# Batch 0's first attention block in a new order: three tokens of q and k first, products of ones in the pauses, g loaded as rows, and the late FFN tiles moved on

## The chip, the cores and the metric

The kernel runs on one core of a Trainium2 chip. Time is the device time of one execution in microseconds; the median of several runs counts. Within the core, TensorE (PE) multiplies matrices and transposes, VectorE (DVE) and ScalarE (ACT) work element by element, GpSimd (POOL) issues most loads and adds, SyncE (SP) issues loads and stores.

## The reference

Squared-relu attention over 8 batches, 12 heads, 448 positions and 64 elements a head, followed by a layer norm and a two-layer FFN with a residual:

```python
scores = (1 / sqrt(64)) * q @ k.T                  # per batch and head
attn   = maximum(scores, 0) ** 2 / 448
x      = (attn @ v), heads side by side            # 8 x 448 x 768
xn     = (x - mean(x)) / sqrt(var(x) + 1e-6) * g   # g: moe_g_ln, 768
out    = x + maximum(xn @ w_ch1, 0) @ w_ch2        # w_ch1 768 x 3072, w_ch2 3072 x 768
```

All inputs and outputs are float32 in HBM.

## The kernel before

**Tiling.** A position is p * 7 + j: 64 values of p on partitions, 7 of j, called tokens or slots here. Each batch is three groups of four heads (G = 3); a group's q and k are tiles of 128 partitions with two rows of 448 elements, and its transposes are 7 pairs of 64x128 blocks for q and as many for k. The loads by POOL's queue cast to bf16 on the way. The 1/std of the layer norm is applied after the second FFN product, so FFN1 needs only the centred x times g (tile xc).

**The first two batches** are worked in two blocks of query tokens each: BLK = (0..2, 3..6) for batch 0, (0..3, 4..6) for batch 1. A block goes over the three groups: transposes (L205 on PE, copies out of PSUM at L209 by DVE and ACT), scores (L307) two key slots at a time, relu on ACT (L318), square on DVE (L296), the product with v (L337), the scaled copy into xT (L344) and, times g, into xc (L350 on DVE; L348 on ACT for groups 1 and 2 of the very first block). At the end `centre` sums over the 768 columns with a product with ones (L385) and subtracts the mean (L391). Then FFN1 of that block (24 tiles `ni` of 128 columns: `ffn1_head` for 0 to 2 at L540, `ffn1` at L518) runs interleaved with the attention units of the next block, by `interleave(main, side, free, ahead)`: it runs `ahead` side units first, then spreads the others over the main units but the last `free`. From batch 2 on both batches of a pair are worked whole; this part isn't touched.

**The order is written by hand** (manual_schedule): each engine runs its instructions in the order in which the program issues them, and waits only where data or a buffer requires it. PSUM has three buffers of two banks (ps_sc: scores, value products, idle_ps) and two of one bank (ps_mm: FFN1 tiles, batch 0's transposes, the busy products).

**Loads.** q and k of batch 0, group 0 come uncast as float32 into `stage` on the queues of SP and ACT (L150), and are cast by DVE (q, tokens 0 to 2), ACT (k) and POOL (q, tokens 3 to 6) at L158. Everything else early goes in order through POOL's queue: q and k of groups 1 and 2, v of groups 0 to 2, the six column blocks of w1 in two halves each (`load_w1`, L138; block i holds tiles 4i to 4i+3), then batch 1's q, k and v (L120). A load on this queue waits for the load eight places before it. g is read as single elements into 128 partitions by six columns, in two loads on SP's queue (L177); `scale_g` (L182, L183) makes g_mean and g_score of it on DVE and is issued before the first block's third unit.

**Products without a use.** `idle(n)` issues n products of 128x128 ones into idle_ps, `busy(n)` n products of 128x448 into a ps_mm buffer. Their results are never read:

```python
idle(30)                                   # before the first transposes
for _ in range(n):                         # busy(n), L283
    nc.tensor.matmul(ps[:, :S], ones, qbuf[0][:, D:D + S], start=True, stop=True)
```

Of the kernel before, what the change touches and what calls it, by code (L numbers as in the profile page):

```python
# [12 lines left out]
def interleave(main, side, free=0, ahead=0):  # L13


    for unit in side[:ahead]:
        unit()
    side = side[ahead:]
    n, done = len(main) - free, 0
    for i, unit in enumerate(main):  # L20
        unit()
        want = min(len(side), (len(side) * (i + 1)) // n)
        while done < want:
            side[done]()
            done += 1
# [3 lines left out]
def kernel(  # L29
# [22 lines left out]
    nc = tc.nc  # L52
    P = 128
    HP = 64
    bf16 = mybir.dt.bfloat16
    fp32 = mybir.dt.float32

    B, H, S, D = q.shape
# [3 lines left out]
    J = S // HP  # L62
    NP = H // 2
    G = NP // 2
# [28 lines left out]
    nc.vector.memset(ones, 1.0)  # L93


    srcs = {
        n: [t[b].rearrange("(r hh) (p j) d -> (hh p) r (j d)", hh=2, p=HP) for b in range(B)]
        for n, t in (("q", q), ("k", k), ("v", v))
# [9 lines left out]
    def load(n, names):  # L108
        if n >= len(groups):
            return  # L110
        b, m = groups[n]
        for name in names:
            if b == 1 and name != "v":
                o = (2 * m + "qk".index(name)) * 2 * S
                t = hold[:, o:o + 2 * S].rearrange("p (r s) -> p r s", r=2)
            elif name == "q":
                t = qbuf[m][:, D:D + 2 * S].rearrange("p (r s) -> p r s", r=2)
            else:
                t = io.tile([P, 2, S], bf16, tag=name, name=name + "_sb", bufs=4 if name == "v" else 3)
            nc.gpsimd.dma_start(t, srcs[name][b][:, m:NP:G, :])  # L120
            qkv[name, b, m] = t
# [21 lines left out]

    stage = hpool.tile([P, K2, S2], bf16, tag="hT", name="stage_sb")
    stage = stage.rearrange("p a n -> p (a n)")[:, :8 * S].bitcast(fp32)
    stage = stage.rearrange("p (i r s) -> p i r s", i=2, r=2)
    for i, (queue, name) in enumerate(((nc.sync, "q"), (nc.scalar, "k"))):
        queue.dma_start(stage[:, i], srcs[name][0][:, 0:NP:G, :])  # L150

    nc.scalar.activation(spool.tile([P, 1], fp32, tag="root", name="root"), eps_sb, ACTF.Sqrt)
    qkv["q", 0, 0] = qbuf[0][:, D:D + 2 * S].rearrange("p (r s) -> p r s", r=2)
# [2 lines left out]
    def cast(copy, name, lo, hi):  # L156
        s = slice(lo * D, hi * D)
        copy(qkv[name, 0, 0][:, :, s], stage[:, "qk".index(name), :, s])  # L158

    load(1, "qk")  # L160
    make_identity(nc, identity)
    load(2, "qk")
    load(0, "v")
    load(1, "v")
    load(2, "v")
    cast(nc.gpsimd.tensor_copy, "q", 3, J)
    for i in range(6):
        load_w1(i)
    load(3, "qkv")
    load(4, "qk")  # L170
    load(5, "qk")

    g_sb = const.tile([P, K1], fp32)
    g_src = moe_g_ln.rearrange("(hf c p) -> hf p c", hf=2, p=HP)
    with nc.allow_non_contiguous_dma(reason="one vector of 768"):
        for hf in range(2):
            nc.sync.dma_start(g_sb[hf * HP:(hf + 1) * HP, :], g_src[hf])  # L177
    g_mean = const.tile([P, K1], fp32)
    g_score = const.tile([P, K1], fp32)

    def scale_g():
        nc.vector.tensor_scalar_mul(g_mean, g_sb, -1.0 / d_model)  # L182
        nc.vector.tensor_scalar_mul(g_score, g_sb, score_scale)  # L183

# [3 lines left out]
    def idle(n):  # L188

        for _ in range(n):  # L190
            nc.tensor.matmul(idle_ps[:, 0, :P], ones, ones, start=True, stop=True)

    xT, xc = {}, {}
    st = {}

    def piece(sb, b, m, n, cuts):
        if b == 0:
            ps = ps_mm.tile([P, 1024], bf16, tag="mm", name="tr_ps")
        else:
            ps = ps_sc.tile([P, 2, 1024], bf16, tag="sc", name="tr_ps")[:, 0]  # L200
        src, i = qkv[n, b, m], "qk".index(n)
        for copy, lo, hi in cuts:
            for j in range(lo, hi):
                for pr in range(2):
                    nc.tensor.transpose(  # L205
                        ps[pr * HP:(pr + 1) * HP, j * P:(j + 1) * P],
                        src[:, pr, j * D:(j + 1) * D], identity)
        for copy, lo, hi in cuts:
            copy(sb[:, i * J + lo:i * J + hi, :],  # L209
                 ps[:, lo * P:hi * P].rearrange("p (j c) -> p j c", c=P))  # L210

    def transposes(b, m):


        if b == 0:
            o = 12 * 1024 + m * 2 * J * P
            sb = early[:, o:o + 2 * J * P].rearrange("p (i c) -> p i c", c=P)
        elif m:
            o = (m - 1) * 2 * J * P
            sb = hold[:, o:o + 2 * J * P].rearrange("p (i c) -> p i c", c=P)  # L220
        else:
            sb = tpool.tile([P, NB, P], bf16, tag="qT", name="qT_sb", bufs=3)
        dve, act = nc.vector.tensor_copy, nc.scalar.copy
        if (b, m) == (0, 0):

            cast(dve, "q", 0, 3)
            cast(act, "k", 0, 3)
            cast(act, "k", 3, J)
            idle(30)
            piece(sb, b, m, "q", ((dve, 0, 3),))  # L230
            idle(2)
            piece(sb, b, m, "k", ((dve, 0, 3), (dve, 3, J)))
            idle(3)
        elif b == 0:
            piece(sb, b, m, "q", ((dve, 0, J),))
            piece(sb, b, m, "k", ((dve, 0, 3), (act, 3, J)))
        else:
            piece(sb, b, m, "q", ((dve, 0, J),))
            piece(sb, b, m, "k", ((dve, 0, J),))
        squares_now()  # L240
        st[b, m] = {
            "q": lambda i, r: sb[:, 0:J],
            "k": lambda i: sb[:, J + i],
            "where": lambda pr, j: (j, pr),
            "attn": [], "sb": sb}
# [25 lines left out]


    FULL = (0, J)
    BLK = (((0, 3), (3, J - 3)), ((0, 4), (4, J - 4)))
    FIRST = (0, BLK[0][0])
    n_early = [0]

    def busy(n):


        ps = ps_mm.tile([P, 512], fp32, tag="mm", name="busy_ps")
        for _ in range(n):
            nc.tensor.matmul(ps[:, :S], ones, qbuf[0][:, D:D + S], start=True, stop=True)  # L283

    def of(blk, b=0):
        o = b % 2 * S
# [4 lines left out]
    def squares_now(n=None):  # L291


        if n is None or n in [k for k, _ in later]:
            for _, a in later:
                nc.vector.tensor_mul(a, a, a)  # L296
            later.clear()
# [99 lines left out]
    def transposed(n):  # L397

        if groups[n][0] < by_dma:
            transposes(*groups[n])  # L400
            return


        if n > by_dma * G:
            load(n + 2, "kq")
        keys_dma(n)
        queries_dma(n)

    def attention_block(b, blk):


        lo, hi, first = b * G, b * G + G, blk[0] == 0
        units = [lambda: transposed(lo)] if first else []

        def unit(n, part):
            squares_now()
            for i in range(4 * part, min(4 * part + 4, J), 2):
                if (b, blk) == FIRST and (n == G - 1 or n and i == 2):
                    busy(1)
                scores(n, tuple(range(i, min(i + 2, J))), blk)  # L420
            if (b, blk) == FIRST and part and n == hi - 1:
                squares_now()
            if b == 1 and not first and part and n == hi - 1:
                transposed(hi)
            if part and n > lo:
                values(n - 1, blk)
                if not first:
                    load(n + 3, "v")
        for n in range(lo, hi):
            units.append(lambda n=n: unit(n, 0))  # L430
            if first and n + 1 < hi:
                units.append(lambda n=n: transposed(n + 1))
            units.append(lambda n=n: unit(n, 1))

        def last():
            if (b, blk) == FIRST:
                piece(st[0, 0]["sb"], 0, 0, "q", ((nc.scalar.copy, 3, J),))
            values(hi - 1, blk)
            if (b, blk) == FIRST:
                busy(2)  # L440
            if b == 1 and not first:
                load(hi + 3, "v")
        units.append(last)
        units.append(lambda: centre(b, blk))
        return units

    def attention(bs):

# [159 lines left out]


    pairs = B // 2  # L610
    for i, unit in enumerate(attention_block(0, BLK[0][0])):
        if i == 2:
            scale_g()
        unit()
    interleave(ffn1_units(0, BLK[0][0]), attention_block(0, BLK[0][1]), 3, 1)
    w2 = wpool.tile([P, K2, d_model], bf16, tag="w2", name="w2")
    for i in range(4):
        load_w2(w2, i, 4)
    load(6, "qkv")
    load(7, "qk")  # L620
    load(8, "qk")
    interleave(ffn1_units(0, BLK[0][1]), attention_block(1, BLK[1][0]), 3, 1)
    interleave(ffn1_units(1, BLK[1][0]), attention_block(1, BLK[1][1]), 3, 1)
    tokens(0)
    transposed(by_dma * G + 1)
# [46 lines left out]
```

## Time and profile before

| | |
|---|---|
| timed runs (3) | median 549.29 us, 549.14 to 549.51 |
| profiled execution | 552.11 us, its span 550.3 us |
| PE busy in the span | 540.8 us |
| DVE, ACT, POOL busy | 266.4, 260.4, 109.5 us |
| HBM read, written | 51.91 MB, 11.01 MB |
| mean granted PE clock | 0.991 |
| first product of FFN1 (L540) | starts at 24.42 us |

The span is counted from the first instruction to the last. An engine's busy time leaves out its waits and its issuing of DMAs; PE's products are pipelined, so that a busy PE needn't be at its peak. PEclk is the share of TensorE's full clock that was granted. All times of instructions below are from the span's start.

### The profile page before, as it was taken

How to read it: one execution, taken by the hardware profiler on the slowest of the kernel's cores; microseconds unless marked ns; L12 is line 12 of the kernel's file. 1: busy time of each engine (PE TensorE's matmuls, PEld its weight loads, DVE VectorE, ACT ScalarE, POOL GpSimd, SP SyncE). 2: the span in 40 equal slices, each digit the busy share in tenths (PEclk: the TensorE clock that was granted, in tenths of full speed). 3: DMA queues.
4: the chain of work that ended last, by engine and by line, in shares of the span. 5: the costliest groups of instructions: out<-in, count | busy, mean ns of one | idle time of the engine just before them, and what ended most of it. 6: DMA issues, size and time to landing. Idle time of an engine off the chain costs nothing.

```text
span 550.3 us, 11108 instructions
## 1 busy us (share of the span) xinstructions
PE 540.8 (98%) x4734; PEld 320.1 (58%) x4734; DVE 266.4 (48%) x511; ACT 260.4 (47%) x424; POOL 109.5 (20%) x135
## 2 busy tenths in 40 slices
PE   6999999999999999999999999999999999999997
PEld 4688778755555555555555555555555555556665
DVE  3686754268897241047787551016687680001111
ACT  3776676565543444455445244445555254440000
POOL 7334102115524200002534400001230400000000
PEclk7899999999999999999999999999999999999999
DMA  9999999999999960018998960005931140001212
GB/s 187 205 206 208 211 170 143 151 165 145 154 157 147 182 53 0 1 30 135 162 168 138 174 115 1 0 15 84 145 81 31 45 101 0 1 0 44 58 43 58
DMA packets 111539, 56.64 MB, mean 103 GB/s; under 512 B 78081, under 2 KB 111489, under 8 KB 111489
## 3 DMA queue, kind: packets, MB, share of 16 engines
q0 software_dynamic: 26976, 25.50, 32.3%
q1 hardware_dynamic: 84000, 29.77, 30.8%
q8 instruction: 37, 0.61, 0.4%
q10 hardware_dynamic: 512, 0.66, 0.3%
q14 instruction: 14, 0.11, 0.1%
HBM read 51.91 MB, written 11.01 MB: 114 GB/s over the span
## 4 chain that ended last, share of the span: by engine, by line
PE 96%; DMA 2%; ACT 1%; DVE 1%; SPq 0%; issue 0%; DVEq 0%
PE o_ps L554 39%; PE h_ps L518 39%; PE sc_ps L307 7%; PE av_ps L337 6%; DMA g_sb<-in_moe_g_ln_dram 2%; PE o_ps L581 1%; PE h_ps L540 1%; PE sum_ps L385 1%; PE tr_ps L205 1%; ACT early L318 1%; DVE early L296 0%; ACT early L209 0%; SPq L177 0%; ACT xc_sb L348 0%; DVE early L209 0%; DVE hT_sb L524 0%
## 5 line engine op out<-in xcount | busy, mean ns | idle before, releaser
L554 PE MATMUL o_ps<-w,hT_sb 128*128 128x384 bf16 x1296 | 219.6, 326 | 0.0
L518 PE MATMUL h_ps<-xc_sb,w 128*128 128x448 bf16 (+2 forms) x1368 | 219.0, 318 | 0.4 <-DVE hT_sb L524 0.4
L518 PEld LDWEIGHTS <-w 128*128 128x128 bf16 x1368 | 128.7, 98 | 86.4 <-issue 2.7
L554 PEld LDWEIGHTS <-hT_sb 128*128 128x128 bf16 x1296 | 123.1, 98 | 93.4 <-issue 15.2
L318 ACT ACTIVATE attn_sb<-sc_ps 128x896 bf16<-128x896 f32 (+4 forms) x150 | 126.4, 902 | 87.8 <-PE sc_ps L307 71.3
L526 ACT ACTIVATE hT_sb<-h_ps 128x448 bf16<-128x448 f32 (+2 forms) x212 | 102.7, 484 | 120.9 <-PE h_ps L518 120.5
L320 DVE TENSOR_TENSOR attn_sb<-attn_sb 128x896 bf16<-128x896 bf16 x126 | 81.7, 653 | 40.3 <-ACT attn_sb L318 39.0
L565 DVE SCALAR_TENSOR_TENSOR o_sb<-o_ps,rstd_sb,xtok_sb 128x384 f32<-128x384 f32 (+1 forms) x57 | 34.4, 604 | 56.4 <-PE o_ps L554 49.8
L503 DVE RECIPROCAL rstd_sb<-rstd_sb 128x1 f32<-128x1 f32 (+1 forms) x10 | 1.7, 168 | 96.6 <-ACT rstd_sb L502 96.6
L368 POOL TENSOR_TENSOR part_sb<-part_sb,xT_sb 128x448 f32<-128x448 f32 x24 | 29.5, 1229 | 69.5 <-DVE xT_sb L344 61.8
L497 DVE BATCH_NORM_STATS2 stats<-xtok_sb 128x6 f32<-128x384 bf16 x56 | 27.5, 533 | 30.4 <-DMA xtok_sb<-xT_sb 30.4
L365 POOL TENSOR_TENSOR part_sb<-xT_sb 128x448 f32<-128x448 bf16 x6 | 6.6, 1104 | 173.7 <-DVE xT_sb L344 144.2
L391 DVE SCALAR_TENSOR_TENSOR xc_sb<-total_sb,g_mean,xc_sb 128x448 bf16<-128x448 f32 (+2 forms) x54 | 29.0, 605 | 20.8 <-ACT total_sb L389 20.8
L307 PE MATMUL sc_ps<-qT_sb,kT_sb 64*64 64x448 bf16 x504 | 35.0, 358 | 0.0
L337 PE MATMUL av_ps<-attn_sb,v_sb 64*64 64x448 bf16 (+2 forms) x672 | 32.3, 327 | 0.0
L344 DVE TENSOR_SCALAR xT_sb<-av_ps 128x896 bf16<-128x896 f32 (+2 forms) x30 | 26.9, 900 | 9.9 <-PE av_ps L337 9.9
L337 PEld LDWEIGHTS <-v_sb 64*64 64x64 bf16 x840 | 23.3, 109 | 10.3 <-issue 1.3
L350 DVE TENSOR_SCALAR xc_sb<-xT_sb,g_sb 128x448 bf16<-128x448 bf16 (+2 forms) x56 | 28.4, 556 | 1.0
L307 PEld LDWEIGHTS <-kT_sb 64*64 64x64 bf16 x504 | 12.1, 105 | 17.6 <-issue 13.3
L120 POOL DMA_DIRECT2D v_sb<-in_v_dram x24 | 17.5, 732 | 22.7 <-PE av_ps L337 19.5
L120 POOL DMA_DIRECT2D k_sb<-in_k_dram x20 | 14.4, 719 | 28.7 <-DMA kT_sb<-k_sb 18.7
L318 ACT ACTIVATE early<-sc_ps 128x768 bf16<-128x768 f32 (+3 forms) x24 | 18.3, 826 | 3.1 <-PE sc_ps L307 3.0
(62 smaller groups left out, 197.7 us busy)
## 6 DMA issues: line engine op xcount, KB each, us to landing
out_dram<-o_sb SPq DMA_DIRECT2D x109, 96.0 KB, 2.2
v_sb<-in_v_dram POOLq DMA_DIRECT2D x24, 224.0 KB, 4.8
w<-in_moe_w_ch_dram POOLq DMA_DIRECT2D x12, 384.0 KB, 14.2
w<-in_moe_w_ch_dram POOLq DMA_DIRECT2D x4, 1152.0 KB, 20.0
q_sb<-in_q_dram POOLq DMA_DIRECT2D x20, 224.0 KB, 7.1
k_sb<-in_k_dram POOLq DMA_DIRECT2D x20, 224.0 KB, 5.9
hold_sb<-in_q_dram POOLq DMA_DIRECT2D x3, 224.0 KB, 11.9
hold_sb<-in_k_dram POOLq DMA_DIRECT2D x3, 224.0 KB, 11.1
```

Source lines behind the costliest of these rows:

```text
L120: nc.gpsimd.dma_start(t, srcs[name][b][:, m:NP:G, :])
L307: nc.tensor.matmul(ps[cols, r, o * w:(o + 1) * w], g["k"](i)[rows, cols], g["q"](i, r)[rows, blk[0]:sum(blk), cols], start=True, stop=True)
L318: nc.scalar.activation(a, ps[:, :, :len(slots) * w], ACTF.Relu)
L320: nc.vector.tensor_mul(a, a, a)
L337: nc.tensor.matmul(ps[cols, hh, :w], v_sb[rows, pr, j * D:(j + 1) * D], g["attn"][i][rows, r, :], start=(j == 0), stop=(j == J - 1))
L350: nc.vector.tensor_scalar_mul(xc[b][:, c, of(blk)], xT[b // 2][:, c, of(blk, b)], g_sb[:, c:c + 1])
L368: nc.gpsimd.tensor_add(part[b], part[b], x[:, c])
L391: nc.vector.scalar_tensor_tensor(xc[b][:, c, of(blk)], total, g_mean[:, c:c + 1], xc[b][:, c, of(blk)], op0=ALU.mult, op1=ALU.add)
L518: nc.tensor.matmul(ps[:, :w], w1[:, c, ni * P:(ni + 1) * P], xc[b][:, c, of(blk)], start=(c == 0), stop=(c == K1 - 1))
L526: nc.scalar.activation(hT[pair][:, ni, o:o + w], ps[:, :w], ACTF.Relu)
L554: nc.tensor.matmul(ps[:, :DH], hT[pair][:, ki, t * P:(t + 1) * P], w2[:, ki, cols], start=(ki == 0), stop=(ki == K2 - 1))
L565: nc.vector.scalar_tensor_tensor(o[:, :w].rearrange("p (c d) -> p c d", d=D), ps[:, :w].rearrange("p (c d) -> p c d", d=D), rstd[pair][:, ...
```

## The change

It does five things.

1. q and k of batch 0, group 0 are loaded in pieces: tokens 0 to 2 of q on SP's queue and of k on ACT's, the rest of k on SP's, the rest of q by POOL's queue with the cast. For groups 1 and 2 the first three tokens of q are loaded ahead of k, the other four behind w1's block 0. Batch 1's first q and k are loaded ahead of w1's block 5.
2. The first block's order is written out in `first_block`. Of q only the three tokens that the block needs are transposed there; the other four of group 0 near its end, those of groups 1 and 2 within the second block (`piece(..., first=False)`, into a ps_sc buffer).
3. `busy(n)` issues products of 128x128 ones, and there are 48 of them in `first_block` in place of 7 of 128x448; `idle` has 32, 3 and 4 in place of 30, 2 and 3.
4. g is loaded as 12 rows of 64 elements in one load on SP's queue, and two float32 products with a 6x6 identity bring it into idle_ps; DVE copies it to g_sb.
5. The last four tiles of the first block's FFN1 (20 to 23) are issued behind three units of the second block's FFN1, and the attention units beside them are spread anew.

```diff
+    load_uncast(nc.sync, "q", 0, FEW)
+    load_uncast(nc.scalar, "k", 0, FEW)
+    load_uncast(nc.sync, "k", FEW, J)
...
+    def load_queries(m, lo, hi):
+        s = slice(lo * D, hi * D)
+        t = qkv["q", 0, m] = qbuf[m][:, D:D + 2 * S].rearrange("p (r s) -> p r s", r=2)
+        nc.gpsimd.dma_start(t[:, :, s], srcs["q"][0][:, m:NP:G, s])
+    load_queries(1, 0, FEW)
+    load(1, "k")
     make_identity(nc, identity)
-    load(2, "qk")
+    load_queries(2, 0, FEW)
+    load(2, "k")
     load(0, "v")
     load(1, "v")
     load(2, "v")
-    cast(nc.gpsimd.tensor_copy, "q", 3, J)
-    for i in range(6):
+    load_queries(0, FEW, J)
+    load_w1(0)
+    load_queries(1, FEW, J)
+    load_queries(2, FEW, J)
+    for i in range(1, 5):
         load_w1(i)
-    load(3, "qkv")
+    load(3, "qk")
+    load_w1(5)
+    load(3, "v")
...
+    g_rows = const.tile([K1, 2, HP], fp32)
+    nc.sync.dma_start(g_rows, moe_g_ln.rearrange("(hf c p) -> c hf p", hf=2, p=HP))
...
     def scale_g():
+        for hf in range(2):
+            nc.tensor.matmul(
+                idle_ps[hf * HP:(hf + 1) * HP, 1, :K1], g_rows[:, hf], identity_g,
+                start=True, stop=True)
+        nc.vector.tensor_copy(g_sb, idle_ps[:, 1, :K1])
...
-            nc.tensor.matmul(ps[:, :S], ones, qbuf[0][:, D:D + S], start=True, stop=True)
+            nc.tensor.matmul(ps[:, :P], ones, ones, start=True, stop=True)
...
+            if not first and b == 0 and n + 1 < hi:
+                units.append(lambda n=n: piece(
+                    st[0, n + 1]["sb"], 0, n + 1, "q", ((nc.vector.tensor_copy, FEW, J),), False))
...
+    def first_block():
+        blk = BLK[0][0]
+
+        def pairs_of_slots(n, *firsts):
+            for i in firsts:
+                scores(n, tuple(range(i, min(i + 2, J))), blk)
+                busy(3)
+        transposed(0)
+        scores(0, (0, 1), blk)
+        piece(st[0, 0]["sb"], 0, 0, "k", ((nc.vector.tensor_copy, FEW, J),))
+        scale_g()
+        busy(4)
+        pairs_of_slots(0, 2, 4, 6)
+        transposed(1)
+        busy(6)
+        pairs_of_slots(1, 0, 2)
+        transposed(2)
+        busy(3)
+        squares_now()
+        scores(1, (4, 5), blk)
+        scores(1, (6,), blk)
+        values(0, blk)
+        squares_now()
+        pairs_of_slots(2, 0, 2)
+        values(1, blk)
+        squares_now()
+        pairs_of_slots(2, 4, 6)
+        squares_now()
+        piece(st[0, 0]["sb"], 0, 0, "q", ((nc.scalar.copy, FEW, J),))
+        values(2, blk)
+        busy(8)
+        centre(0, blk)
...
-    interleave(ffn1_units(0, BLK[0][0]), attention_block(0, BLK[0][1]), 3, 1)
+    first_block()
+
+    units = ffn1_units(0, BLK[0][0])
+    interleave(units[:-4], attention_block(0, BLK[0][1]), 1, 1)
...
-    interleave(ffn1_units(0, BLK[0][1]), attention_block(1, BLK[1][0]), 3, 1)
+    late, units = units[-4:], ffn1_units(0, BLK[0][1])
+    interleave(units[:3] + late + units[3:], attention_block(1, BLK[1][0]), 3)
```

More of the change, by code (lines that the diff above doesn't have):

```diff
@@ L93 @@
     nc.vector.memset(ones, 1.0)
+    BLK = (((0, 3), (3, J - 3)), ((0, 4), (4, J - 4)))
     srcs = {
@@ L148, with load_uncast @@
     stage = stage.rearrange("p (i r s) -> p i r s", i=2, r=2)
-    for i, (queue, name) in enumerate(((nc.sync, "q"), (nc.scalar, "k"))):
-        queue.dma_start(stage[:, i], srcs[name][0][:, 0:NP:G, :])
+    FEW = BLK[0][0][1]
+    def load_uncast(queue, name, lo, hi):
+        s = slice(lo * D, hi * D)
+        queue.dma_start(stage[:, "qk".index(name), :, s], srcs[name][0][:, 0:NP:G, s])
+    load_uncast(nc.sync, "q", 0, FEW)
+    load_uncast(nc.scalar, "k", 0, FEW)
+    load_uncast(nc.sync, "k", FEW, J)
     nc.scalar.activation(spool.tile([P, 1], fp32, tag="root", name="root"), eps_sb, ACTF.Sqrt)
@@ L158, in cast @@
         copy(qkv[name, 0, 0][:, :, s], stage[:, "qk".index(name), :, s])
-    load(1, "qk")
+    def load_queries(m, lo, hi):
+        s = slice(lo * D, hi * D)
+        t = qkv["q", 0, m] = qbuf[m][:, D:D + 2 * S].rearrange("p (r s) -> p r s", r=2)
+        nc.gpsimd.dma_start(t[:, :, s], srcs["q"][0][:, m:NP:G, s])
+    load_queries(1, 0, FEW)
+    load(1, "k")
     make_identity(nc, identity)
-    load(2, "qk")
+    load_queries(2, 0, FEW)
+    load(2, "k")
     load(0, "v")
@@ L165 @@
     load(2, "v")
-    cast(nc.gpsimd.tensor_copy, "q", 3, J)
-    for i in range(6):
+    load_queries(0, FEW, J)
[3 more added lines that the diff above has]
+    for i in range(1, 5):
         load_w1(i)
-    load(3, "qkv")
+    load(3, "qk")
+    load_w1(5)
+    load(3, "v")
     load(4, "qk")
     load(5, "qk")
+    g_rows = const.tile([K1, 2, HP], fp32)
+    nc.sync.dma_start(g_rows, moe_g_ln.rearrange("(hf c p) -> c hf p", hf=2, p=HP))
     g_sb = const.tile([P, K1], fp32)
[L174 to L177, printed above, removed]
     g_mean = const.tile([P, K1], fp32)
     g_score = const.tile([P, K1], fp32)
+    identity_g = const.tile([K1, K1], fp32)
     def scale_g():
+        for hf in range(2):
[3 more added lines that the diff above has]
+        nc.vector.tensor_copy(g_sb, idle_ps[:, 1, :K1])
         nc.vector.tensor_scalar_mul(g_mean, g_sb, -1.0 / d_model)
@@ L194, with piece @@
     st = {}
-    def piece(sb, b, m, n, cuts):
-        if b == 0:
+    def piece(sb, b, m, n, cuts, first=True):
+        if b == 0 and first:
             ps = ps_mm.tile([P, 1024], bf16, tag="mm", name="tr_ps")
@@ L224, in transposes @@
         if (b, m) == (0, 0):
+            nc.vector.tensor_copy(identity_g, identity[:K1, :K1])
             cast(dve, "q", 0, 3)
@@ L228, in transposes @@
             cast(act, "k", 3, J)
[L229 to L232, printed above, removed]
+            idle(32)
+            piece(sb, b, m, "q", ((dve, 0, FEW),))
             idle(3)
+            piece(sb, b, m, "k", ((dve, 0, FEW),))
+            idle(4)
         elif b == 0:
-            piece(sb, b, m, "q", ((dve, 0, J),))
+            piece(sb, b, m, "q", ((dve, 0, FEW),))
             piece(sb, b, m, "k", ((dve, 0, 3), (act, 3, J)))
@@ L273 @@
     FULL = (0, J)
-    BLK = (((0, 3), (3, J - 3)), ((0, 4), (4, J - 4)))
     FIRST = (0, BLK[0][0])
@@ L417, in unit @@
             for i in range(4 * part, min(4 * part + 4, J), 2):
-                if (b, blk) == FIRST and (n == G - 1 or n and i == 2):
-                    busy(1)
                 scores(n, tuple(range(i, min(i + 2, J))), blk)
-            if (b, blk) == FIRST and part and n == hi - 1:
-                squares_now()
             if b == 1 and not first and part and n == hi - 1:
@@ L432, in attention_block @@
                 units.append(lambda n=n: transposed(n + 1))
+            if not first and b == 0 and n + 1 < hi:
+                units.append(lambda n=n: piece(
+                    st[0, n + 1]["sb"], 0, n + 1, "q", ((nc.vector.tensor_copy, FEW, J),), False))
             units.append(lambda n=n: unit(n, 1))
         def last():
-            if (b, blk) == FIRST:
-                piece(st[0, 0]["sb"], 0, 0, "q", ((nc.scalar.copy, 3, J),))
             values(hi - 1, blk)
-            if (b, blk) == FIRST:
-                busy(2)
             if b == 1 and not first:
@@ L610 @@
     pairs = B // 2
[L611 to L614, printed above, removed]
-    interleave(ffn1_units(0, BLK[0][0]), attention_block(0, BLK[0][1]), 3, 1)
+    first_block()
+    units = ffn1_units(0, BLK[0][0])
+    interleave(units[:-4], attention_block(0, BLK[0][1]), 1, 1)
     w2 = wpool.tile([P, K2, d_model], bf16, tag="w2", name="w2")
```

## Prediction

> **What bounds the kernel now.** First the page: TensorE is the bound of the whole.
>
> ```profile
> PE 540.8 (98%) x4734; PEld 320.1 (58%) x4734; DVE 266.4 (48%) x511; ACT 260.4 (47%) x424; POOL 109.5 (20%) x135
> ```
>
> Of the 9.5 us in which PE stands still, about 6 lie before 29.4 us and the rest behind its last product; the answer on PE's waits from 32 us on is empty. So whatever moves the end of batch 0's first block moves the end of the kernel one for one, as long as the weights keep up. Next, the chain of waits of the first 60 us (start, length, what):
>
> ```profile
> 2.05 9.12 DMA g_sb<-in_moe_g_ln_dram
> ...
> 11.27 0.34 DVE g_mean L182
> ...
> 12.33 0.59 ACT early L209
> 12.92 0.72 ACT early L318
> ...
> 23.92 0.56 PE sc_ps L307 x16
> 24.48 1.98 PE h_ps L540 x18
> ```
>
> The reader is to see that the chain begins with the load of g: DVE stands in order, and its g_mean waits until 11.2. The waits of the first 32 us show what queues behind it:
>
> ```profile
> ACT early L209 <- DVE early L209: 3.9, 2, 3.0
> DVE g_mean L182 <- DMA g_sb<-in_moe_g_ln_dram: 3.6, 1, 3.6
> ```
>
> ACT, which must do the block's relus, idles 9.28 to 12.33. FFN1 (L540) starts at 24.42. Third, the clock: it is 0.50 from 7.74 to 17.98, which is three times 3.41 us. Cut into such stretches (PE busy, granted clock):
>
> ```profile
> 0.92:4.33 3.41, 3.24 (x30) 1.00 0.67 204
> 4.33:7.74 3.41, 1.93 (x43) 1.00 1.25 194
> 7.74:11.15 3.41, 2.69 (x48) 0.50 1.31 198
> 11.15:14.57 3.42, 2.07 (x31) 0.50 1.26 205
> 14.57:17.98 3.41, 3.41 (x66) 0.50 1.24 205
> 21.39:24.81 3.42, 2.47 (x49) 1.00 1.24 207
> ```
>
> A stretch with 1.93 busy is followed by half clock, one with 3.41 by full clock, and one with 2.47 keeps it. Of the 1.93, 1.00 are transposes (L205 alone in the same stretches: 1.00, 1.91, 0.42, 1.28, last 0). Fourth, POOL's timeline, where each w load waits for the load eight places earlier, and so tells when that landed:
>
> ```profile
> 13.23 0.66 POOL L138 DMA_DIRECT2D w<-in_moe_w_ch_dram  x1 [0.46 <-DMA v_sb<-in_v_dram]
> 15.72 0.66 POOL L138 DMA_DIRECT2D w<-in_moe_w_ch_dram  x1 [1.84 <-DMA v_sb<-in_v_dram]
> 24.25 0.66 POOL L138 DMA_DIRECT2D w<-in_moe_w_ch_dram  x1 [1.29 <-DMA w<-in_moe_w_ch_dram]
> 28.02 0.72 POOL L120 DMA_DIRECT2D hold_sb<-in_k_dram  x1 [1.17 <-DMA w<-in_moe_w_ch_dram]
> 31.89 0.71 POOL L120 DMA_DIRECT2D hold_sb<-in_q_dram  x1 [1.24 <-DMA w<-in_moe_w_ch_dram]
> ```
>
> Column blocks 1, 2 and 3 of w1 (tiles ni 4-7, 8-11, 12-15) are complete at 24.25, 28.02 and 31.89, block 4 at 35.67, block 5 near 39.7; tiles 4, 8, 12 and 16 start near 26.9, 30.6, 33.5 and 38.1. The weights have 1.6 to 2.7 us in hand: a gain beyond that is capped by them.
>
> **The change, part by part.**
>
> *First tokens.* q and k of group 0 come as 3 of 7 tokens first: 0.39 MB lie ahead of the first cast instead of 0.92. The DMA answer gives 0.40 MB/us there, so 1.3 us less, less some 0.3 for shorter rows: cast at 4.2 instead of 5.12. Then cast 0.58, six q transposes, copy, six k transposes, copy (0.36 each), by their rows: first scores at 6.0 instead of 7.36, first relu 6.4 instead of 7.77. The rest of k follows on SP's queue (lands near 5.0, cast 0.61, eight transposes, copy): second relu near 7.6.
>
> *g as rows.* 768 elements become 12 rows of 256 B, third on SP, near 5.4; needed at 6.6. Two tiny fp32 products and one DVE copy of 128x6 are new. No fp32 product is in the trace: between 0.03 (a transpose) and 0.56 us (the longest half-clock product) each; I take 0.1, since they have six columns; the copy 0.2. PE is in order, so a late g would now stop scores, not just DVE. Removed: the 3.6 us stand of DVE and ACT's 3.0 behind it.
>
> *New order.* What is left is ACT's chain: nine relus at 0.70 start to start, three at 0.45, three copies at 0.48, four multiplications by g at 0.33: 10.4 us. From 6.4 without a gap: 16.8. Laying the three engines' orders beside each other with these steps (DVE squares 0.47, xT 0.50, value products 0.77 a group, transposes 0.034 each) leaves ACT waiting about 0.5 for the rest of k, 0.5 and 0.6 for group 1's and 2's k copies, 0.7 for xT of group 1 (behind DVE's squares) and 0.7 for that of group 2, 3.0 in all. First FFN1 product near 20.0. The same laying out of the order before, with its landings and clock, gives 24.84 where the trace has 24.42, so I take 19.7: 4.7 us earlier.
>
> *Products in the pauses.* 48 products of 128x128 of ones replace 7 of 128x448. At full clock I price them 0.056 (half the 0.113 of the 30 cold ones), 2.7 us in all, under ACT's chain; they cost nothing while ACT is last. Counting them, 4.33:7.74 gets 2.6 us busy (2.0 without transposes) against 1.93 (0.93), the next two 3.1 and 2.8, and 14.57:17.98 some 2.0. The level that keeps the clock lies between 1.93 and 2.47 (without transposes 0.93 and 2.47). I take the clock as kept. If one stretch is lost, FFN1 comes 1.3 later, two 2.6. The Trainium skill (TensorE: Matmul & The Clock Gate, Why this matters for your kernels) asks only that no gap between bursts exceed about 3 us. The trace differs: clock 0.50 after a stretch whose longest gap was 1.3 us; by that rule the order before would have run at full clock too, and the fillers would be worth nothing. Its Part 4 holds that transposes do not count as busy; the trace neither proves nor refutes it.
>
> *Late q transposes.* Two pieces of eight move from groups 1 and 2 into the second block: 2 x 0.28 = 0.56 us on a busy PE, and two DVE copies of 0.41, where DVE and ACT are about 90% busy (32 to 40 us): 0.3 more, from 0 to 0.8. PE's 0.36 us stand on DVE at 29.4 is gone or moves: I count it gone.
>
> *Loads and late tiles.* POOL's cast of q goes, three q loads split (same bytes), and q, k of batch 1 go ahead of w1 block 5. In the DMA answer for 5 to 9 us, 773 software packets take 110.8% of 16 engines, 92 ns each; 745 of g's take 20.1%, 17 ns each. So g costs 0.8 us on all engines and more on the slowest: by my estimate 1.4 of the lag seen in the gap between v loads (13.23 to 15.72, where 1.12 is usual). Linear between those two packet prices, a split load takes 0.3 more than a whole one, 0.9 for three; the earlier start gives 0.4. Blocks 1 to 4 land 0.9 earlier: 23.3, 27.1, 31.0, 34.8. Tile 4 would be due at 19.7 + 2.03 (head) + 0.57 + 0.28 = 22.6: waits 0.7. Tile 8 is 3.3 behind (four tiles at 0.57, 28 scores): 26.6, waits 0.5. Tile 12, 3.8 behind: 30.9, waits 0.1. Tile 16, 4.1 behind: 35.1, none. Block 5 lands 2 x 1.12 - 0.9 later than before, 41.1; tiles 20-23, moved behind three units of the next FFN1, come near 41. Three units now precede batch 1's first transposes, whose inputs land earlier: nothing.
>
> *Sum.* 4.7 + 0.36 - 0.56 - 0.3 - 1.3 = 2.9 us. The profiled execution took 552.11 (span 550.3, 1.8 around it) and would take 549.2. The median of the timed runs, 549.29, is 2.8 lower; the same 2.9 off gives **546.4**.
>
> **The rivals.**
>
> *Half clock for a while.* One or two stretches fall below the level: FFN1 at 21.0 to 22.3. The waits for w1 then vanish, so 546.4 to 547.7, middle 547.1. For it: only 2.0 busy without transposes. Against: 2.6 with them.
>
> *The lag is not g's.* Then blocks land at 24.8, 28.6, 32.5, 36.3; tile 4 waits 2.2, tile 8 0.5, tile 12 0.1: gain 1.4, 547.9. For it: the lag grew by 1.3 at v1, where g's elements were all in. The Trainium skill (DMA: Bandwidth & Descriptors, Latency and other measured facts) says two of the 16 engines are usually slower; no view here names engines.
>
> *The change gives nothing.* Lag stays and short rows cost what full rows do (five pieces at 1.12 for three): blocks 1.3 later still, block 1 at 26.2; waits 4.1, gain 0.1: 549.2. The same page (Specifications) asks for 512 B rows for line rate, and the first pieces write 384 B; no run here shows such rows.
>
> *Slower.* PE becomes the bound: after 7.74 the clock stays at half past 21.39 because no stretch reaches the level. The fillers cost 0.113 each, 2.7 more, on a PE that is then last; FFN1 starts at 25.1 and its head still runs at half clock. With the moved transposes: 1.2 slower, 550.5. It decides only if three full stretches in a row are not enough; 14.57:17.98 in the trace, one full stretch, was.
>
> **How the numbers follow.** Forecast 0.52, half clock 0.18, lag 0.16, nothing 0.08, slower 0.06. A measurement of this kernel tells about 0.2% (1.1 us) from no change. Faster: 0.52 + 0.18 + 0.16 = 0.86; same 0.08; slower 0.06. The low end, 544.8, is the forecast without its 1.3 us of w1 waits and with 0.3 less in the second block; the high end, 548.4, is the lag case with 0.5 us more on DVE.
>
> **What would show it.** Right: no DVE wait over 1 us on g; first relu near 6.4; clock 1.00 from 4.33 on; FFN1's first product near 19.7; short PE waits on w at 22 to 27 us; PE's waits empty after 32. Wrong: PE waiting for g; half clock after 7.74; PE waits on w summing to over 2.5 us, or any at tile 20; a stand of PE on DVE or ACT between 20 and 42 us over 1 us.

## Result: 2.7 us slower, and the profile after

The changed kernel takes 552.04 us (median of 6 runs, 551.38 to 552.50), the kernel before 549.37 beside it (549.14 to 549.57). The ratio is 1.0043, with a 95% interval of 1.0033 to 1.0054: by the medians it is 2.7 us slower, where 2.9 us less was forecast. The profiled execution took 551.95 us, its span is 550.2 us.

The page's first line has PE 1.2 us busier than before, in a span that is as long:

```profile
PE 542.0 (99%) x4783; PEld 321.2 (58%) x4783; DVE 267.4 (49%) x516; ACT 260.6 (47%) x423; POOL 111.0 (20%) x137
```

The clock did not fall in the first block, as was forecast, but it rose late. In the same stretches as before (length, PE busy, products, granted clock) the view gives 1.00 throughout; the first two that were in question:

```profile
4.33:7.74 3.41, 3.41 (x47) 1.00 1.28 165
7.74:11.15 3.41, 3.35 (x70) 1.00 1.18 171
```

The next three stretches hold 2.91, 3.24 and 2.64 us busy. The 1.00 of the first row is not a full clock, though. The trace's record of the clock begins with its first change, at 7.06 in this profile, and the view gives 1.00 for whatever lies ahead of that. The lengths of equal products tell the pace there; four products of ones ahead of 7.06 and four behind it (start, length, what):

```profile
5.97 0.61 PE L217 MATMUL idle_ps<-ones 128*128 128x128 bf16 x4
...
7.55 0.40 PE L309 MATMUL busy_ps<-ones 128*128 128x128 bf16 x4
```

In a row they start 0.107 us apart ahead of 7.06, and 0.056 us apart behind it. So PE ran at half pace until 7.06 here; in the profile before it did so until 4.34, where that record begins.

No wait for g is left among the waits of the first 32 us, and ACT, which stood 3.0 us before a copy of k, now waits 1.4 us at most once q and k of group 0 are cast, for its first scores.

The first product of FFN1 (now L597) starts at 21.10, 3.32 us earlier than in the profile before. And yet the last product of the second FFN (o_ps) starts at 546.34, only 0.13 earlier than its 546.47. So nearly all of the 3.3 us is lost again behind 21 us. The chain of waits of the first 48 us (start, length, what) shows where:

```profile
6.22 7.26 DMA v_sb<-in_v_dram
...
14.44 13.41 DMA w<-in_moe_w_ch_dram
...
29.54 1.20 DVE early L322 x2
...
33.58 1.95 ACT early L344 x2
```

The chain no longer runs through the first block at all: until 27.86 it is the loads of v and w1, then DVE's squares, ACT's relus and DVE's centring in the second block. PE's waits from 20 to 46 us name the same releasers (where it waited, for whom: total, times, longest); before, this answer held 0.9 us for ACT at the first block's sums, 0.4 for DVE at 29.4, and nothing behind that:

```profile
PE h_ps L575 <- DMA w<-in_moe_w_ch_dram: 0.8, 2, 0.6
PE h_ps L597 <- DVE xc_sb L417: 0.5, 1, 0.5
PE av_ps L363 <- DVE early L322: 0.4, 1, 0.4
PE av_ps L363 <- ACT early L344: 0.3, 1, 0.3
```

POOL's timeline gives the landings of w1, as before, by the loads that wait for them:

```profile
24.29 0.70 POOL L123 DMA_DIRECT2D hold_sb<-in_k_dram  x1 [1.18 <-DMA w<-in_moe_w_ch_dram]
...
28.14 0.66 POOL L141 DMA_DIRECT2D w<-in_moe_w_ch_dram  x1 [1.28 <-DMA w<-in_moe_w_ch_dram]
```

Blocks 1 and 2 are complete at 24.29 and 28.14 (block 0, by the same view, at 18.33 and block 3 at 31.93), where 23.3, 27.1 and 31.0 were forecast for blocks 1 to 3.

### The profile page after: what moved, and what is told of

Its sections match the earlier page's. It is cut to its first block, busy times and chain, and to the rows that moved or that the text cites. A ratio compares the mean times of both kernels' runs of the same rounds, so it can differ in the third digit from the quotient of the medians.

```text
span 550.2 us, 11208 instructions
## 1 busy us (share of the span) xinstructions
PE 542.0 (99%) x4783; PEld 321.2 (58%) x4783; DVE 267.4 (49%) x516; ACT 260.6 (47%) x423; POOL 111.0 (20%) x137
## 4 chain that ended last, share of the span: by engine, by line
PE 93%; DMA 4%; POOL 1%; DVE 1%; ACT 0%; issue 0%; POOLq 0%
PE o_ps L611 39%; PE h_ps L575 38%; PE sc_ps L333 6%; PE av_ps L363 6%; DMA w<-in_moe_w_ch_dram 2%; PE o_ps L638 1%; DMA v_sb<-in_v_dram 1%; PE h_ps L597 1%; PE sum_ps L411 1%; PE tr_ps L231 0%; ACT early L344 0%; DVE early L322 0%; POOL k_sb L123 0%; POOL v_sb L123 0%; POOL q_sb L173 0%
## 5 line engine op out<-in xcount | busy, mean ns | idle before, releaser
L376 DVE TENSOR_SCALAR xc_sb<-xT_sb,g_sb 128x448 bf16<-128x448 bf16 (+2 forms) x56 | 29.4, 576 | 1.0
L333 PEld LDWEIGHTS <-kT_sb 64*64 64x64 bf16 x504 | 12.1, 105 | 17.6 <-issue 13.3
```

Of the source, the lines that this page charges most:

```text
L333: nc.tensor.matmul(ps[cols, r, o * w:(o + 1) * w], g["k"](i)[rows, cols], g["q"](i, r)[rows, blk[0]:sum(blk), cols], start=True, stop=True)
L376: nc.vector.tensor_scalar_mul(xc[b][:, c, of(blk)], xT[b // 2][:, c, of(blk, b)], g_sb[:, c:c + 1])
```

## The experiments

The theories: the profile before is not typical of the kernel before, so the gain was counted from a base that the timed runs do not have; and behind FFN1's start the change loses time to three things of its own, the split loads of q, the late transposes, and the late tiles. The rival: the first block still sets the end one for one, and something in it (g, the fillers, the first tokens) went wrong.

Each experiment is compared with runs of the kernel before beside it. Their medians were 549.62 to 549.67, against 549.37 beside the changed kernel, so a difference of two times below carries up to 0.3 us from this alone; the ratios do not.

### The kernel before, again

The same file, to see whether the half clock of its profile is usual.

> The kernel before once more, to see whether its profiled execution (552.11, half clock from 7.74 to 17.98) stands for its timed runs (549.3). Theory A, the clock: timed runs don't lose the clock, and another profile shows full clock, FFN1's first product near 21.6 instead of 24.42 and a span near 547.5. Theory B, the profiler: profiling costs this kernel 2.8 us whatever the clock; another profile shows half clock again, FFN1 at 24.4 and a span near 550.3.

It took 549.44 us (549.25 to 551.23, 10 runs), ratio 0.9996 (0.9984 to 1.0008). Its profiled execution took 549.4 us with a span of 547.6, 2.7 us less than in the profile before. Its record of the clock has one change in the first 60 us, to full at 9.21, and no fall. Ahead of it PE ran at half pace, as the lengths of fourteen equal transposes show, first in this profile, then in the profile before:

```profile
6.55 0.96 PE L205 MATMUL tr_ps<-identity,k_sb 128*64 128x128 bf16 x14
```

```profile
6.27 0.64 PE L205 MATMUL tr_ps<-identity,k_sb 128*64 128x128 bf16 x14
```

Fourteen transposes also took 0.96 us in the profile before at 8.34, where its granted clock is 0.50. So neither execution ran all of its first block at full clock. In the profile before the clock rose at 4.34, fell at 7.75 and was back at 17.99; here it rose at 9.21 and stayed, although the stretch that follows holds only 2.22 us busy of 3.42 (9.21 to 12.63). DVE's wait for g is less than half as long:

```profile
DVE g_mean L182 <- DMA g_sb<-in_moe_g_ln_dram: 1.5, 1, 1.5
```

FFN1 starts at 21.75 instead of 24.42, and everything behind it is 2.67 us earlier too (last o_ps starts at 543.80 against 546.47). The half clock is only a part of this. In both executions the chain runs through the load of g, which ends at 9.62 here and ended at 11.17 before, and ACT's copy behind it begins at 10.80 instead of 12.33. So by the chain 1.53 of the 2.67 us are there at that copy, and the other 1.1 come behind it, where the profile before was at half clock. The weights land earlier as well, block 1 at 22.86, block 2 at 26.64 and block 3 at 30.65:

```profile
22.86 0.66 POOL L138 DMA_DIRECT2D w<-in_moe_w_ch_dram  x1 [1.30 <-DMA w<-in_moe_w_ch_dram]
```

All experiments together have 93 timed runs of the kernel before, with a median of 549.6. One had a mean granted clock of 0.991, as in the profile before, and took 551.82 us. Three others took over 551.2 us: 551.23 at 0.994, and 551.84 and 551.81 at 0.996. So the profile before shows a rare execution. That the half clock makes an execution long is not shown: 32 runs have a mean of 0.996 or 0.997, which is what one stretch of 3.41 us at half clock leaves (0.996 in the profile of the next experiment), and a median of 549.7, against 549.6 for the 58 runs at 0.999 or 1.000. Against this one the changed kernel starts FFN1 0.65 us earlier and ends 2.54 us later: it loses 3.2 us behind FFN1's start. In the stretch from 21 to 45 us PE is busy 23.63 us here and 22.03 in the changed kernel, though the latter's holds 0.8 us of transposes more. That is 1.6 us of stands, 0.8 of transposes, and 0.33 by which the second FFN1 head is drawn out (2.47 us instead of 2.14); the last 0.5 are not told apart.

The Trainium skill (TensorE: Matmul & The Clock Gate, Part 1, What's actually happening) says that the window over which the clock is decided runs free of the kernel, so that the point of the change varies from run to run, by 0.5 us either way. The two profiles of one file agree with the first and go beyond the second: the clock rises at 4.34 in one and at 9.21 in the other.

### Only g as rows

```diff
-            nc.sync.dma_start(g_sb[hf * HP:(hf + 1) * HP, :], g_src[hf])
+    nc.sync.dma_start(g_rows, moe_g_ln.rearrange("(hf c p) -> c hf p", hf=2, p=HP))
...
+        nc.vector.tensor_copy(g_sb, idle_ps[:, 1, :K1])
```

The kernel before with the change's fourth part alone.

> The kernel before with g loaded as 12 rows and turned by two products, nothing else of the change. If g's wait is what stands at the head of the path (the prediction's reading): 0.5 to 3 us faster than before. If the timed runs wait for g no more than 1 us: within 0.3 us of before. DVE's wait for g gone in its profile in either case; if g's 768 elements cause the loads' lag, block 1 of w1 lands 0.8 to 1.4 us earlier than in the profile before.

549.86 us (549.32 to 550.88, 10 runs), ratio 1.0001 (0.9990 to 1.0011): g's wait is gone and nothing is won. w1's block 1 landed at 22.32, 0.54 earlier than in the kernel before run again. Two executions of that kernel lay 1.39 us apart at this landing (24.25 and 22.86), so it is not shown what g's elements cost the other loads; no run shows the 1.4 us that the prediction put down to them. FFN1 starts at 21.70 against 21.75. In this profile PE ran at half clock for one stretch (7.59 to 11.00). The seven timed runs with a mean clock of 1.000 took 549.8 to 550.9, so the half clock hides no gain.

### Late tiles undone

```diff
-    units = ffn1_units(0, BLK[0][0])
-    interleave(units[:-4], attention_block(0, BLK[0][1]), 1, 1)
+    interleave(ffn1_units(0, BLK[0][0]), attention_block(0, BLK[0][1]), 3, 1)
...
-    late, units = units[-4:], ffn1_units(0, BLK[0][1])
-    interleave(units[:3] + late + units[3:], attention_block(1, BLK[1][0]), 3)
+    interleave(ffn1_units(0, BLK[0][1]), attention_block(1, BLK[1][0]), 3, 1)
```

The changed kernel with the old spreading, and w1's block 5 ahead of batch 1's q and k again.

> The changed kernel with the late tiles and the spreading of the second block undone (tiles 20 to 23 stay in their place, w1's block 5 ahead of batch 1's q and k). If the new spreading overloads DVE and ACT (PE stands 1.9 us between 30 and 42 us in the changed kernel): 1 to 2 us faster than the changed kernel, about 550.5. If the weights' arrival sets the end there: the same as the changed kernel or up to 1 us slower.

551.87 us (551.59 to 554.07, 6 runs), ratio 1.0046 (1.0029 to 1.0063): nothing is given back. FFN1 starts at 20.29 here. The first block is that of the changed kernel; in this execution the clock rose at 4.34 instead of 7.06, and the first relu came at 6.30 instead of 7.09. PE then stands for the weights; the stretch with that stand has 1.55 us busy and is followed by one at half clock:

```profile
PE h_ps L574 <- DMA w<-in_moe_w_ch_dram: 1.9, 1, 1.9
```

```profile
21.39:24.81 3.42, 1.55 (x17) 1.00 1.24 208
24.81:28.20 3.39, 3.39 (x26) 0.50 1.25 203
```

Only two of the six timed runs show a fall of the clock (552.86, the profiled one, and 554.07); the other four took 551.6 to 551.9, so the half clock is not what keeps the time up. An early first block runs into the weights, and with the split loads in place the late tiles aren't the only thing that costs.

### q of groups 1 and 2 whole

```diff
-    load_queries(1, 0, FEW)
+    load_queries(1, 0, J)
...
-            piece(sb, b, m, "q", ((dve, 0, FEW),))
+            piece(sb, b, m, "q", ((dve, 0, J),))
```

The changed kernel with q of groups 1 and 2 loaded at once (their second loads behind w1's block 0 left out, group 2's changed alike) and transposed whole in the first block.

> The changed kernel with q of groups 1 and 2 loaded and transposed whole in the first block. If the pieces moved into the second block cost their PE time and DVE's two copies there: 0.6 to 1.5 us faster than the changed kernel. If the first block takes back as much (ACT last there): the same within 0.3 us.

550.35 us (549.88 to 550.61, 10 runs), ratio 1.0011 (1.0002 to 1.0020): 1.7 us of the 2.7 are gone. FFN1 starts 0.48 us later (21.58), blocks 1, 2 and 3 land at 22.92, 27.12 and 30.84, and PE's waits hold no wait for w1; that for the centred tile (L415 here, 0.5 us) is still there.

### Both undone

> The changed kernel with both undone: q of groups 1 and 2 loaded and transposed whole, and tiles 20 to 23, the spreading and w1's block 5 in their old places. What is left of the change is the first block's order, its first tokens, its products of ones and g as rows. If the loss lies in the second block's new order (centre's DVE chain uncovered, 0.9 us) and in the q pieces (about 1.7): no slower than before, 549.0 to 549.5, with PE waiting for DVE ahead of the second FFN1 head gone. If the first block itself costs: near 550.3, as with whole q alone.

With the late tiles undone as well, 549.46 us (549.23 to 549.92, 11 runs), ratio 0.9997 (0.9988 to 1.0006). This kernel keeps the new first block, the first tokens of group 0, the fillers and g as rows: together they are worth nothing that the runs can tell. Its FFN1 starts at 21.35.

### Whole loads, late transposes kept

> The changed kernel with q of groups 1 and 2 in one load each, but its last four tokens still transposed in the second block. It parts the price of the split loads from that of the moved transposes. If the split loads hold back w1 (its blocks land 1.2 us later than with whole q): near the whole-q kernel, 550.4 to 550.9. If the pieces in the second block are the price (16 transposes on PE, two copies on DVE, two more score buffers): within 0.4 us of the changed kernel, about 551.6 to 552.

The loads of the kernel with q whole, but the transposes of the four late tokens stay in the second block: 550.76 us (550.23 to 551.05, 10 runs), ratio 1.0019 (1.0010 to 1.0028). So of the 1.7 us, 1.3 are the splitting of two loads (552.04 to 550.76) and 0.4 the late transposes (550.76 to 550.35). The first step is clear of noise; the intervals of the other two kernels overlap, so that 0.4 alone is not.

### The centre covered

```diff
-    interleave(units[:3] + late + units[3:], attention_block(1, BLK[1][0]), 3)
+    interleave(units[:3] + late + units[3:], attention_block(1, BLK[1][0]), 3, 1)
```

In the kernel before, batch 1's first 28 transposes ran between the sums and the second FFN1 head, and covered DVE's chain to the centred tiles. The change moved them behind the head. The edit moves them back, in three kernels.

> The changed kernel, in which batch 1's first transposes are issued ahead of the second block's FFN1 head again, as in the kernel before; nothing else differs. Theory 'uncovered centre' (in the changed kernel the second block's FFN1 head stands behind DVE's centred tiles, L417, since nothing is left to run beside them): PE's stand of 0.5 us on DVE's xc tile is gone, the head of 18 products takes 1.98 us again instead of 2.30, no tile near 40 us takes 1.1 us; time about 0.9 us below the changed kernel's 552.0, so 551.1. Rival 'the late tiles' spreading costs it' (attention units beside the first block's FFN1 sit more tightly): the stand on DVE goes but the time stays at 551.8 to 552.0, PE waiting on squares or on w1 in its place.

550.85 us (550.25 to 552.01, 10 runs), ratio 1.0022 (1.0013 to 1.0032): 1.2 us less than the changed kernel. PE's timeline (start, length, what) has the transposes ahead of the head, no wait in front of it, and the head at its old length:

```profile
40.84 0.97 PE L231 MATMUL tr_ps<-identity,hold_sb 128*64 128x128 bf16 x28
41.74 2.14 PE L597 MATMUL h_ps<-xc_sb,w 128*128 128x256 bf16 x18
```

In the changed kernel the same place reads:

```profile
41.41 2.47 PE L597 MATMUL h_ps<-xc_sb,w 128*128 128x256 bf16 x18 [0.49 <-DVE xc_sb L417]
```

The stand of 0.49 and the 0.33 by which the head is longer make 0.82 of the 1.2. POOL's timeline of this kernel also prices the split loads one by one:

```profile
18.89 0.66 POOL L141 DMA_DIRECT2D w<-in_moe_w_ch_dram  x1 [1.04 <-DMA w<-in_moe_w_ch_dram]
19.88 0.66 POOL L141 DMA_DIRECT2D w<-in_moe_w_ch_dram  x1 [0.34 <-DMA q_sb<-in_q_dram]
20.87 0.66 POOL L141 DMA_DIRECT2D w<-in_moe_w_ch_dram  x1 [0.33 <-DMA q_sb<-in_q_dram]
```

The two late pieces of q land 0.99 us apart from the load ahead of them and from each other; with the late tiles undone it was 0.94 and 1.08. Whole loads of this size, 224 KB, landed 1.12 apart in the profile before (v1 and v2), so four sevenths of one would be 0.64 by bytes.

> The changed kernel with q of groups 1 and 2 in one load each, their late transposes kept in the second block (550.76 us by itself), and with batch 1's first transposes ahead of the second FFN1 head. If split loads and the uncovered centre are all that costs time, this keeps what the change meant to win, 0.56 us of transposes out of the first block, and pays them back in the second: 549.5 to 549.9, within 0.1% of the kernel before. If moving transposes wins anything in itself, it comes in below 549.2.

With whole loads and the late transposes: 549.93 us (549.74 to 550.58, 12 runs), ratio 1.0003 (0.9995 to 1.0012). Its profiled execution, 550.55 us, lies at the slow end of its runs (w1's block 1 at 24.06), so only the timed runs are used.

> The changed kernel with q of groups 1 and 2 loaded and transposed whole in the first block (550.35 us by itself), and with batch 1's first transposes ahead of the second FFN1 head. Theory 'uncovered centre': it gives back what separates it from the kernel with late tiles undone too (549.46), so 549.4 to 549.6, equal to the kernel before. Rival 'spreading': 550.2 to 550.4, unchanged.

With q whole: 549.59 us (548.87 to 550.12, 12 runs), ratio 0.9996 (0.9987 to 1.0005). PE's waits for the centre and for w1 are gone, and from 21 to 45 us it is busy 23.63 us, as in the kernel before; this profiled execution, 548.87, is the fastest of its runs. So the whole loss is accounted for by timed runs alone: 552.04 to 550.85 (centre covered, 1.2), to 549.93 (whole loads, 0.9), to 549.59 (transposes moved back, 0.3). The ratios go the same way, 1.0043, 1.0022, 1.0003 and 0.9996. The intervals part the first two steps; they overlap for the last.

### Without the fillers

`busy` returns at once, so that the 48 products of ones aren't issued.

> The changed kernel without the 48 products of ones of its first block (the 39 ahead of it stay). If they keep the clock, as the prediction has it: half clock for one or two stretches in its records, FFN1 1.3 to 2.6 us later, and the time the same or up to 1 us slower, since the weights set the pace behind. If the clock doesn't need them: the same clock, and within 0.3 us.

551.63 us (551.23 to 552.20, 4 runs), ratio 1.0038 (1.0024 to 1.0051). FFN1 starts at 20.56, 0.54 earlier; but the clock rose 1.6 us earlier too, at 5.44, so this does not tell what the fillers cost. The clock falls at 19.09. Cut at that point, the stretch ahead of the fall has 1.65 us busy:

```profile
15.68:19.09 3.41, 1.65 (x38) 1.00 1.32 201
19.09:22.51 3.42, 3.35 (x31) 0.50 1.24 206
```

Three of these four runs have a mean granted clock of 0.996 or 0.997, and all six of the changed kernel 1.000. So the fillers do keep the clock, and it brings nothing in time: 551.63 lies within the range of the changed kernel's own runs.

### The first tokens alone

The kernel before with three tokens of q and k of group 0 loaded first, and the order of the first block left as it was.

```diff
+    load_uncast(nc.sync, "q", 0, 3)
+    load_uncast(nc.scalar, "k", 0, 3)
+    load_uncast(nc.sync, "k", 3, J)
...
-    cast(nc.gpsimd.tensor_copy, "q", 3, J)
+    nc.gpsimd.dma_start(t[:, :, o], srcs["q"][0][:, 0:NP:G, o])
```

> The kernel before with only group 0's first three tokens of q and k loaded first (and the other four of q by POOL's queue). If the start of the loads sets the first block: 0.7 to 1.2 us faster. If g's element load (now behind two loads on SP) or ACT's chain takes it back: within 0.3 us; FFN1's first product then stays near 21.7.

554.54 us (554.38 to 554.87, 4 runs), ratio 1.0092 (1.0076 to 1.0107). This answers another question than it asked: the products of `busy` read 448 columns of q, the late tokens among them, and so PE waited for POOL's load:

```profile
PE busy_ps L289 <- DMA q_sb<-in_q_dram: 4.2, 1, 4.2
```

With `busy` reading 192 columns of the first tokens:

> The kernel before with q and k of batch 0's group 0 loaded in pieces, three tokens first, the rest of k on SP's queue and of q by POOL's, and with the busy products reading 192 columns of those three tokens, where an earlier kernel of this study read 448 columns and so made PE wait for POOL's load. Theory 'the weights' arrival is the floor': the first product of FFN1 comes 0.7 to 1.1 us earlier than in the kernel before (20.7 to 21.1 where that ran at full clock), yet the time is 549.0 to 549.6, since w1's blocks land no earlier and PE then waits for them. Rival 'the first block sets the end one for one', as the prediction had it: 548.4 to 548.9.

550.45 us (549.59 to 551.02, 10 runs), ratio 1.0012 (1.0003 to 1.0021). Both expectations missed. FFN1 did not come earlier but at 23.30, for a third reason: with the order unchanged, PE reaches the transposes of the rest of k before it has landed.

```profile
PE tr_ps L210 <- DMA k_sb<-in_k_dram: 1.5, 1, 1.5
```

It waits another 1.2 us for the copy behind them. The clock rose at 6.81 here, and the stretch from there to 10.22, with the first of these stands, has 1.81 us busy and is followed by half clock from 10.22 to 17.05. So the test of whether the weights are a floor under an earlier first block failed. What bears on that is the stand of 1.9 us for w1 where FFN1 began at 20.29. That the pieces of the change need each other (first tokens, order, fillers) is shown only for this one combination.

## Why the prediction was wrong, point by point

**The base.** "The median of the timed runs, 549.29, is 2.8 lower; the same 2.9 off gives 546.4": this step failed first and cost most. The 2.8 us were no constant offset. They lie ahead of FFN1, which starts 2.67 us earlier in an execution of 549.4 us: 1.53 of them up to ACT's first copy, behind a load of g that landed later, and the rest behind it, at half clock. Of the forecast 4.7 us, 2.67 were already in the median that the gain was taken from.

The forecast missed the measured time by 5.6 us. It counts up to 2.67 for the base, 1.4 for the first block (FFN1 at 21.10 instead of 19.7), and 1.4 for what is lost behind FFN1's start (3.2 instead of 1.8, which is 4.7 - 2.9). The rest, 0.1, is within the spread of the runs.

**The first block.** Its mechanisms came as forecast: no wait for g, first cast at 4.08 (forecast 4.2), and no fall of the clock. Its sizes did not. The first relu came at 7.09 instead of 6.4, and from there to FFN1 it took 14.0 us instead of 13.3, so FFN1 began at 21.10 instead of 19.7. The first 0.7 is the clock's late rise: the prediction took "clock 1.00 from 4.33 on" from the profile before, and the rise came at 7.06. Where it came at 4.34 with the same first block (late tiles undone), the first relu stood at 6.30 and FFN1 at 20.29, again 14.0 us later. The other 0.7 was missing in the sum of ACT's chain. What is left of 4.7 is 4.7 - 2.67 - 1.4 = 0.6. "Removed: the 3.6 us stand of DVE and ACT's 3.0 behind it": in the second execution of the kernel before the stand on g is 1.5 us, and with it gone alone FFN1 begins 0.05 earlier. Group 1's transposes and copies are late next: the copy of k that ACT waited for began at 10.76 there and at 10.80 before.

**The split loads.** "A split load takes 0.3 more than a whole one, 0.9 for three; the earlier start gives 0.4", and g 1.4 back: blocks 0.9 earlier than in the profile before. Block 1 came at 24.29, where that profile has 24.25. What g's elements were worth is not shown, and the late pieces of q took 0.94 to 1.08 each where 0.64 would go by bytes. The interpolation between two packet prices was the wrong row: the nearest load of the same kind, 1.12 for a whole one, was the better guide, and it stood among the rivals ("short rows cost what full rows do") with 0.08. Whole loads of just two of the three give back 0.9 to 1.3 us of time.

**Waits for w1.** Forecast 1.3 us, found 0.8 at tiles 4 and 8. That the size is near is luck: the weights were 1.0 us later than assumed, and the products 1.4.

**Late transposes.** 0.56 us of PE were forecast, and 0.8 us busy are in the trace; moved back they give 0.3 to 0.4 us, in two pairs of kernels whose intervals overlap. That they give less than 0.8 because the first block then has to do them is not shown.

**DVE and ACT in the second block, 0.3, and the 0.36 at 29.4.** PE's wait on hT at 29.4 did go. Waits for relus and squares of 0.3 and 0.4 us stand at 35 and 38 instead, and 0.5 for the centre at 41. None of them is the single stand over 1 us that the prediction named as a sign of being wrong, but they sum to 1.1, and empty waits behind 32 us were its sign of being right.

**"Three units now precede batch 1's first transposes, whose inputs land earlier: nothing."** The sentence looked at the transposes' inputs, and not at what the transposes had covered. This cost 0.8 to 1.2 us, and is what turned a change that is level with before into a slower one, together with the loads.

**The rivals.** The half-clock rival put FFN1 at 21.0 to 22.3, and 21.10 came, but not by its mechanism: no stretch fell below the level, the rise was late. The slower case through half clock did not occur either. "The lag is not g's" was half right: the same element loads were there in the execution with block 1 at 22.86. The case on the other side was looked for in the clock, and it lay in the second block. The rule of the Trainium skill (TensorE: Matmul & The Clock Gate, Why this matters for your kernels) names only idle gaps over about 3 us as losing the clock. It is contradicted once more: with the late tiles undone, 0.50 followed a stretch whose longest stand was 1.9 us.

## What to carry to other kernels

Before a gain is taken from a profile, ask whether the profiled execution is the one that was timed: an excess of its time over the median (here 2.8 us) is a symptom with a place, and the gain may lie in that place. Ahead of the clock's first recorded change, read the pace from the lengths of equal products and not from the granted clock. When instructions are moved, price what they covered where they stood, not only what they wait for where they go. A load cut in pieces should be priced by the nearest whole load of its kind, not by bytes.

## What the runs showed of the hardware

Ahead of the first recorded change of the clock the view gives 1.00 while equal products ran at half pace (0.107 us apart against 0.056). In the 14 profiles the rise to full lies between 4.04 and 9.21 us, and in two of the same file at 4.34 and 9.21. From the rise on the clock changed at multiples of 3.41 us. Cut there, the stretches at full clock that were followed by half clock hold 1.29 to 1.93 us of PE busy (six profiles, longest stands 0.8 to 1.9 us), and the thinnest that kept it, in the first 80 us, holds 2.22. Without the transposes this order would not hold: 2.22 less 0.90 kept the clock, and 1.54 without any transposes lost it. So the transposes seem to count as busy.

Four sevenths of a q load take 0.94 to 1.08 us where a whole load takes 1.12. And an execution's weights can land 1.4 us later with nothing changed (block 1 at 24.25 and at 22.86 in two profiles of the kernel before), so the landings of a single profile do not settle what a load costs; the timed runs did.
